# A new written order of all steps, pinned on five engines instead of three, in a decaying linear attention followed by a gated convolution

## The chip, the cores and the metric

The kernel runs on one core of one Trainium2 chip. The metric is the device time of one execution in microseconds. Three runs of the kernel before took 331.88, 332.5 and 334.31 us, a median of 332.5 us. One more execution was profiled; durations, waits and windows come from that one.

## What is computed

The first half is a linear attention with a complex decay for 4 batches, 8 heads, 768 time steps and a head dimension of 48. The second half treats the 8 x 48 = 384 outputs of a time step as channels, runs a causal convolution of 5 taps over them as a gate, and multiplies the gate into a projection:

```python
mag = np.sqrt(a_re * a_re + a_im * a_im)
scale = np.minimum(mag, 0.999) / (mag + 1e-06)
a_re_n, a_im_n = (a_re * scale, a_im * scale)
for t in range(S):
    ar, ai = (a_re_n[:, :, t, :, None], a_im_n[:, :, t, :, None])
    new_re = ar * S_re - ai * S_im
    new_im = ar * S_im + ai * S_re
    kv = np.einsum('bhd,bhe->bhde', k[:, :, t], v[:, :, t])
    S_re, S_im = (new_re + kv, new_im)
    y[:, :, t] = np.einsum('bhd,bhde->bhe', q[:, :, t], S_re)
...
for k in range(K):
    gate_pre += conv_w[k][None, None, :] * xp[:, k:k + S, :]
gate = 1.0 / (1.0 + np.exp(-gate_pre))
val = x @ w_val
return (gate * val @ w_out).astype(np.float32)
```

All data is float32, except that the three weight arrays arrive as 64-bit floats.

## The kernel before, in words

The kernel does not run the recurrence step by step. It takes the logarithm of the decay, sums it along time, and turns k and q into decayed and rotated vectors of 96 components, so that the attention becomes matrix products over chunks of 128 time steps with a carried state.

**Units and chunks.** The work of the attention is cut into 10 units: 8 of a batch with four heads, of which the first and the last are split into two of two heads each. Units 0 and 1 are two heads each, units 2 to 7 four, units 8 and 9 two. A unit has six chunks of 128 steps.

**Steps.** Every stream of work is a Python generator, and a letter stands for one advance of one generator. In the order of the data:

- `L` loads one of ar, ai, k or q of a unit through SyncE (line 114, two transfers each); the seventh and eighth `L` load the raw 64-bit weights w_val and w_out (line 141). `V` loads v of a unit (line 132, three transfers).
- `W` turns the weights into float32 on VectorE with one ScalarE instruction each (lines 186 to 208); the conv weights are loaded in the course of it (line 223).
- `X` and `x` (even and odd units) prepare a unit: logarithm and exponential on ScalarE (lines 278, 282, 289, 292, 297), VectorE lines 284, 294 and 299. `R`/`r` take the arctangent (312), sum along time (249), and form the angle in turns (318, 328, 332). `A`/`a` add the sum of the logarithms (344, 348). `S` is the two sines (356, 360), `E` the two exponentials (365, 367).
- `B` multiplies k and q by the decay (379) and the rotation (382) into kx and, for q, into the tile trig; kx goes out to DRAM as kd (line 392, SyncE). There is one kx buffer, so line 382 for the next unit waits until TensorE has transposed the last.
- `N` loads half a unit of kd back as kn, with time on the partitions (line 413, three transfers, after a small GpSimd memset in line 407). `T` transposes kx and trig on TensorE (430), and ScalarE copies each result into kq (431).
- Per chunk, `s` makes the scores (457, 458), `k` masks them on VectorE (464), `y` makes the output from the carried state and the scores (477, 480) and copies it out on ScalarE (481), and `t` updates the state (494, 495, copy in 497). There is one PSUM bank for y.
- `D` moves three chunks of y of all heads of a unit into xT, the array with channels on the partitions (line 509, issued by GpSimd).
- `C` is the conv on VectorE for 128 channels of a batch (518, then 521 four times), `G` the sigmoid on ScalarE (529), `M` the projection in pieces of 384 time steps (matmuls recorded as line 255; 542 multiplies the gate in; 576 copies the result), `O` the store of 128 time steps by GpSimd (813). For the last batch the conv is done in halves, and the projection of a piece begins before the gate is there.

**Table sets.** ScalarE holds the functions of one table set at a time. `table_set` (line 104) loads another set if the last loaded one has a different name: one for logarithm and exponential (`X`, `E`), one for the trigonometric functions (`R`, `S`), one for the sigmoid (`G`). The written order of these steps therefore decides how many loads there are.

**What sets the order.** The string `ORDER` holds 991 letters. A loop calls `advance` once for each letter, then goes round a fixed list of letters until all is done. A letter whose conditions are not met does nothing:

```python
for key in ORDER:
    advance(key)
while not finished():
    assert any([advance(key) for key in "TskGMBEASRXaxrCWtyDONVL"])

before = {}
for ins in nc.cur_bb.bb.instructions:
    if ins.engine not in IN_ORDER:
        continue
    if ins.engine in before:
        tc.add_manual_dep(
            ins, before[ins.engine].name,
```

The framework under the kernel chooses the order of an engine's instructions itself where nothing ties them. The last loop ties every instruction of an engine in `IN_ORDER` to the one written before it on that engine, so that these engines run the written order. In the kernel before these are TensorE, ScalarE and VectorE. SyncE and GpSimd, which issue the transfers, run in the framework's order.

**Buffers that decide when a transfer may be issued.** Six buffers hold the loads (a load waits until the one six before it has been read), three hold kn, two v, two trig, one kx, four z, two xT (the raw weights use the same two), two the outputs before their store. TensorE has four general PSUM banks, two for scores, one for the state and one for y.

Of the kernel before, what the change touches and what calls it, by code (L numbers as in the profile page):

```python
# [19 lines left out]

PI = math.pi
ORDER = (
    "LLXLXxxXXVxXLxxXXxxXRxrWWWWWLRWWRrrLWLVWRARRALWrarWraARSSWWWaWWWWWrSSEWEBBBLBWXWXEENXLNWTTTWTTWT"
    "XTXTBLsskBXBWkyLWtBTskNXXLtRRxRyWskWWsWxTTxTRykWtRTxWxWxTWWTyLsWkWRtWTxytskxrrDyAttWsksARNSyktSr"
    "DVysWtrAErysWrkWDErBLatBskSatBLyLSkaNByXEWWXyNWTTtDTTTTTTLTWTTTTXTTTtEstBLXsVBktkyXWsBLkWyBskxtX"
    "yDstykWskNXytxWCCCCCTTXTyTTDTTTTxCCTCTTTTVTCTsktCxskCCLCCtNyCxCskCRRCLGMRMMsxtMykMxMyDRAARRsxrrr"
    "ktRSSMMAOMMstrEEOryMrMBLMMrSSBNyaMBLLLOaXMtkXMMaMyMEMDBTTTTTTTTTTTTXTTXTTstEBLMsNtBkykBLxsOMxsNt"
    "yVksXBkXtCysxkXtXyMxMkyxTTTyttTOCTTTTTCTTCTCMDDCOTNxTCTCTCCCCLRCCRCskRstCxCCGMMMMMMRskRtVykLRxrr"
    "rMMORsykAMSyrDMSAAEaOrskrtMrMsOaEBMtLBNykMSyMaMtSEBLLXyBNXMMTTMTTTTTTLTTTTTTTTsEtMXDBLsXBkkBLXLx"
    "txXyskCtysBXMOtCXRRyDskRxkCNtTtTVTTTTTTsxxRAyLRxCkCMANxRxrrAyMMMMOyDtTVTTTTTrTTRSSssCCktCyskCras"  # L30
    "kECtOyCCsEBkrBCCtCCyDBskCtykNCGMaMaMMyMtByMCCCMMOCCCtTDTTTTTTTMsksrtrCNCSMVMCSskMMykOMCMMEEBCOsB"
    "NsBtNMykMMCykMDyMstBTTTTTOTTkTtstykMyDssMtykkMMOtMCCyCsCksCtCCCCCCCOykDCtCCMGCCMstyMMCGMMyMkyMMt"
    "MDMOOMMMMMOCCCCCCGMMMMMMMMOOMMO"
)
IN_ORDER = (
    mybir.EngineType.PE, mybir.EngineType.Activation, mybir.EngineType.DVE
)
TURN = 2.0 ** 24
RADIAN = 2.0 * PI / 2.0 ** 32 * (1.0 - 2.0 ** -22)
# [962 lines left out]
```

## Time and profile before

| what | value |
|---|---|
| median of three runs | 332.5 us (331.88 to 334.31) |
| the profiled execution's own time | 332.24 us |
| its span, first to last instruction | 330.5 us |
| mean granted TensorE clock | 0.940 |
| moved by transfers | 53.31 MB, 161 GB/s on average |
| ScalarE table loads | 31 |

The page names engines as PE (TensorE matmuls), PEld (its weight loads), DVE (VectorE), ACT (ScalarE), POOL (GpSimd), and SPq for the queue of SyncE, which only issues transfers. A group row reads: line, engine, operation, output<-input, shapes, count, then busy us and mean ns of one, then the idle time of the engine just before those instructions and who ended it. A wait row reads: engine and line, `<-` what released it, us in total, how many times, the longest. A window row reads: start and end, its length, then for PE, PEld, DVE, ACT and POOL the busy us and the number of instructions, then the granted clock, the busy share of the transfer engines and GB/s. A timeline or chain row begins with the start and the duration in us. A row of transfer issues reads: the transfer, the queue, the count, KB each, and the median us from issue to landing.

### The profile page before, as it was taken

The page shows a single profiled execution, that of the slowest core. Times are in us where ns is not written, and L with a number is a line of the kernel's source. Part 1 is how long each engine was busy: PE and PEld are TensorE (multiplying, and loading weights), DVE is VectorE, ACT ScalarE, POOL GpSimd, SP SyncE. Part 2 cuts the span into 40 slices and gives each one's busy share as a digit, 9 for nine tenths or more (in the row PEclk, how much of TensorE's full clock was granted, in tenths as well). Part 3 has the DMA queues.
Part 4 walks back from the last instruction along what each step waited for, and adds up shares of the span by engine and source line. Part 5 has one row for each costly group of instructions (what it writes and reads, how often), then busy time and mean ns, then how long its engine had stood idle before and what let it go on. Part 6 is the DMA issues. An engine that isn't in the chain of part 4 may idle for free.

```text
span 330.5 us, 8134 instructions
## 1 busy us (share of the span) xinstructions
PE 263.2 (80%) x3234; PEld 204.1 (62%) x3234; DVE 257.4 (78%) x341; ACT 245.9 (74%) x455; POOL 59.8 (18%) x148
## 2 busy tenths in 40 slices
PE   0030775747999899989969999899998999999950
PEld 0030664635998487668868887698696756866520
DVE  4499889999698999968968999689789857294500
ACT  5729879999979789998849899989894474552110
POOL 3000001121033022030430030303303312132110
PEclk9999959785999799999969999999999999999995
DMA  7994989839999722788989025997424504321120
GB/s 198 279 244 100 264 235 241 173 91 285 237 322 168 195 77 69 236 227 225 278 224 189 3 68 194 246 275 184 122 57 126 137 18 125 84 86 32 60 78 0
DMA packets 87804, 53.31 MB, mean 161 GB/s; under 512 B 36432, under 2 KB 84816, under 8 KB 87760
## 3 DMA queue, kind: packets, MB, share of 16 engines
q1 hardware_dynamic: 83664, 43.28, 50.8%
q0 software_dynamic: 4096, 9.44, 9.4%
q8 instruction: 27, 0.44, 0.6%
q14 instruction: 17, 0.14, 0.1%
HBM read 33.83 MB, written 14.16 MB: 145 GB/s over the span
## 4 chain that ended last, share of the span: by engine, by line
PE 31%; DVE 23%; ACT 14%; issue 12%; DMA 11%; POOL 3%; SPq 2%; POOLq 0%; DVEq 0%; ACTq 0%
PE pt L430 9%; PE pv L255 6%; PE po L255 4%; DMA kn<-kd 4%; ACT L104 3%; PE sc_ps L457 3%; DVE sm L464 3%; PE y_ps L480 3%; DMA raw<-in_moe_w_val_dram 3%; DVE main L379 3%; DMA kd<-kx 3%; DVE main L249 2%; DVE main L318 2%; DMA xT<-y_sb 2%; PE y_ps L477 2%
## 5 line engine op out<-in xcount | busy, mean ns | idle before, releaser
L431 ACT COPY kq<-pt 96x384 f32<-96x384 f32 x128 | 52.0, 508 | 4.7 <-PE pt L430 4.5
L509 POOL DMA_DIRECT2D xT<-y_sb x80 | 41.0, 519 | 77.4 <-ACT y_sb L481 74.9
L521 DVE SCALAR_TENSOR_TENSOR z<-xT,cw_sb,z 128x768 f32<-128x768 f32 (+1 forms) x60 | 51.4, 856 | 1.7
L255 PE MATMUL pv<-xT,wv_sb 128*64 128x384 f32 x288 | 51.4, 499 | 0.0
L255 PE MATMUL po<-wo_sb,z 128*64 128x384 f32 x288 | 51.2, 488 | 0.0
L430 PE MATMUL pt<-ident,kx 128*96 128x128 f32 x192 | 37.2, 308 | 10.4 <-DVE kx L382 9.5
L464 DVE TENSOR_TENSOR sm<-sc_ps,mask 128x512 f32<-128x512 f32 (+1 forms) x60 | 34.6, 578 | 13.0 <-PE sc_ps L458 9.0
L480 PE MATMUL y_ps<-sm,v_in 128*48 128x128 f32 x384 | 41.5, 279 | 3.1 <-DVE sm L464 3.1
L457 PE MATMUL sc_ps<-kq 96*64 96x128 f32 x384 | 42.4, 281 | 1.8 <-DVE sm L464 1.7
L458 PE MATMUL sc_ps<-kq 96*64 96x64 f32 x384 | 42.3, 227 | 0.0
L477 PE MATMUL y_ps<-kq,S_sb 96*48 96x128 f32 x320 | 36.3, 286 | 7.2 <-ACT y_sb L481 4.1
L104 ACT ACT_TABLE_LOAD x31 | 39.8, 1283 | 1.3 <-PEq L986 0.8
L430 PE MATMUL pt<-ident,trig 128*96 128x128 f32 x192 | 36.5, 305 | 4.5 <-DVE trig L382 2.8
L458 PEld LDWEIGHTS sc_ps<-kq 96*64 96x64 f32 x384 | 38.5, 140 | 1.7
L255 PEld LDWEIGHTS pv<-xT,wv_sb 128*64 128x64 f32 x288 | 26.0, 141 | 17.6 <-issue 2.9
L457 PEld LDWEIGHTS sc_ps<-kq 96*64 96x64 f32 x384 | 32.1, 141 | 5.1 <-DVE sm L464 2.6
L255 PEld LDWEIGHTS po<-wo_sb,z 128*64 128x64 f32 x288 | 24.6, 136 | 15.4 <-DVE z L542 1.6
L481 ACT COPY y_sb<-y_ps 112x256 f32<-112x256 f32 (+1 forms) x60 | 19.5, 326 | 19.6 <-PE y_ps L480 19.0
L430 PEld LDWEIGHTS pt<-ident,kx 128*96 128x96 f32 x192 | 23.5, 142 | 15.2 <-issue 11.7
L477 PEld LDWEIGHTS y_ps<-kq,S_sb 96*48 96x48 f32 x320 | 21.3, 125 | 15.1 <-ACT y_sb L481 6.4
L480 PEld LDWEIGHTS y_ps<-sm,v_in 128*48 128x48 f32 x384 | 27.1, 126 | 4.1 <-DVE sm L464 3.9
L494 PE MATMUL S_ps<-v_in,kn 128*64 128x48 f32 x320 | 27.7, 225 | 1.6 <-ACT S_sb L497 1.6
(84 smaller groups left out, 484.5 us busy)
## 6 DMA issues: line engine op xcount, KB each, us to landing
kd<-kx SPq DMA_DIRECT2D x12, 576.0 KB, 5.0
out_dram<-ot POOLq DMA_DIRECT2D x24, 192.0 KB, 2.5
ar_in<-in_a_re_dram SPq DMA_DIRECT2D x12, 288.0 KB, 4.3
ai_in<-in_a_im_dram SPq DMA_DIRECT2D x12, 288.0 KB, 4.7
k_in<-in_k_dram SPq DMA_DIRECT2D x12, 288.0 KB, 4.1
q_in<-in_q_dram SPq DMA_DIRECT2D x12, 288.0 KB, 4.1
xT<-y_sb POOLq DMA_DIRECT2D x48, 72.0 KB, 3.3
v_in<-in_v_dram SPq DMA_DIRECT2D x16, 144.0 KB, 4.9
```

Source lines behind the costliest of these rows:

```text
L104: nc.scalar.preload_act_table_set(name)
L255: nc.tensor.matmul(out[c:c + 64], lhsT[:, c:c + 64], rhs, **kw)
L430: nc.tensor.transpose(pt[:C2, j, :], src[:, j, f, h, :], ident)
L431: nc.scalar.copy(tj[:, s, f], pt[:C2].rearrange("c j p -> c p j"))
L457: nc.tensor.matmul(sc[lo:lo + half, h, :], k[:, :half], q, start=True, stop=True)
L458: nc.tensor.matmul(sc[hi:hi + half, h, half:], k[:, half:], q[:, half:], start=True, stop=True)
L464: nc.vector.tensor_tensor(out=two(sm), in0=two(sc[:, :g]), in1=mask[:, :, None, :].to_broadcast([C, 2, g // 2, C]), op=ALU.mult)
L477: nc.tensor.matmul(o, self.S_sb[n - 1][:, h * D:(h + 1) * D], self.part(1, h, n), start=True, stop=False)
L480: nc.tensor.matmul(o, vt[:, h, n], sm[:, h, :], start=(n == 0), stop=True)
L494: nc.tensor.matmul(S_all[:64, cols], kn[:, c0:c0 + 64], vt[:, h, n], **at_h)
L509: XQ.dma_start(out=xTs[b][c0 % P:c0 % P + c2 - c0, c0 // P, EXT + hf * HS:EXT + (hf + 1) * HS], in_=self.y[hf][r0:r0 + c2 - c0, h // 2],)
L521: nc.vector.scalar_tensor_tensor(out=z, in0=xT[:, c, EXT + t0 - t:EXT + t0 - t + n], scalar=cw_sb[:, TAPS - 1 - t, c:c + 1], in1=z, op0=AL ...
```

## The change

The whole string `ORDER` is replaced by another one of the same length, with the same number of each letter, and `IN_ORDER` gains SyncE and GpSimd. Nothing else in the kernel differs: the code of every step, the tiles and the buffers are the same, but steps stand in another order, and the transfers of SyncE and GpSimd are issued in the written order too.

```diff
 ORDER = (
-    "LLXLXxxXXVxXLxxXXxxXRxrWWWWWLRWWRrrLWLVWRARRALWrarWraARSSWWWaWWWWWrSSEWEBBBLBWXWXEENXLNWTTTWTTWT"
-    "XTXTBLsskBXBWkyLWtBTskNXXLtRRxRyWskWWsWxTTxTRykWtRTxWxWxTWWTyLsWkWRtWTxytskxrrDyAttWsksARNSyktSr"
-    "DVysWtrAErysWrkWDErBLatBskSatBLyLSkaNByXEWWXyNWTTtDTTTTTTLTWTTTTXTTTtEstBLXsVBktkyXWsBLkWyBskxtX"
-    "yDstykWskNXytxWCCCCCTTXTyTTDTTTTxCCTCTTTTVTCTsktCxskCCLCCtNyCxCskCRRCLGMRMMsxtMykMxMyDRAARRsxrrr"
-    "ktRSSMMAOMMstrEEOryMrMBLMMrSSBNyaMBLLLOaXMtkXMMaMyMEMDBTTTTTTTTTTTTXTTXTTstEBLMsNtBkykBLxsOMxsNt"
-    "yVksXBkXtCysxkXtXyMxMkyxTTTyttTOCTTTTTCTTCTCMDDCOTNxTCTCTCCCCLRCCRCskRstCxCCGMMMMMMRskRtVykLRxrr"
-    "rMMORsykAMSyrDMSAAEaOrskrtMrMsOaEBMtLBNykMSyMaMtSEBLLXyBNXMMTTMTTTTTTLTTTTTTTTsEtMXDBLsXBkkBLXLx"
-    "txXyskCtysBXMOtCXRRyDskRxkCNtTtTVTTTTTTsxxRAyLRxCkCMANxRxrrAyMMMMOyDtTVTTTTTrTTRSSssCCktCyskCras"
-    "kECtOyCCsEBkrBCCtCCyDBskCtykNCGMaMaMMyMtByMCCCMMOCCCtTDTTTTTTTMsksrtrCNCSMVMCSskMMykOMCMMEEBCOsB"
-    "NsBtNMykMMCykMDyMstBTTTTTOTTkTtstykMyDssMtykkMMOtMCCyCsCksCtCCCCCCCOykDCtCCMGCCMstyMMCGMMyMkyMMt"
-    "MDMOOMMMMMOCCCCCCGMMMMMMMMOOMMO"
+    "XLXLLXXXXxxXxXxxRLxRRxWRWWWLAWRWLRxrALWLWrrAWWRSSErrWEBVBLNaXBLXraWBTaNWWrSSWWWWTWTWVTXTTTETWsWW"
+    "sXXWWkskstEBBLWWyXWBBWkWTWLLWtXtXRRRWyWkWtTWxxxTNTLTytWtskRRRAWxxytTTxRyxAskWTskNyDxryskAStrrskD"
+    "SsWykrrarWEtWrVytEBWLSDBtskStBLNLBaLysNakTXyXTTTETTTTTTTTWTWTTETBLsWyDtWsXBkktWyXstyWBLVsXksyNDx"
+    "BtXTTkTTkystXyTkWxWCCCCTTyDXCTVTtTTxTNTTCTTsskRykstCtCCxCxCCCsLCkyCCtRCRCGMMMtxMkMRAAMRxyDttRsxr"
+    "rMrAsRSMSMrOEMkLyrMrMOaMEBLMOBMkarSaBSByLLTXMNyMXMTTTLMTTTTTTTTTTEENTTsMXXsMXtkDyBMsLBkyktsyBLtx"
+    "NksxVCBkystkCMTTytxxTODtXTyDCCVXCTTCxTMMtTTMLXTxTTCLCTTTxOCCTsCCCkCCRRRNCstCOCGMMMMMRkMRysRtMxrr"
+    "ryAMAsRkSAMtOrarSEskrykaDMEBLMMMrBayMBLSyBtMNMMSXMNsLLETTMTTTTTTXkyTDTTTTTTXtXETBLssktyXsktytsBk"
+    "XkBLxxtOBXyNXRsRCtyskkTTCTTVtxRTTTTyCOMxxyDMRTOTNRTLTVRTCTRCxTTsskkDtyxsktAxrrsCrtSykSAMALEEBBNs"
+    "BBraaMrNOyMyMstTTaMCCrDkCTTrTTTCkCSCTtyCCtCCCOCGMMMyMDCssktMskSECVMtyskCEBMstCCCMOBNCNykMyBMMkys"
+    "MtBTTDCTkOTTTTTtCCyMMyCDtMskstMMMstkMykCMsMOtyMMOystkMsOMDMCCCCtCCytCCCCkCCkCMMMCCCGMOCCMGyMMMyM"
+    "MODMOMMMMMOCCCCCCMGMMMMOMMOMMOM"
 )
 IN_ORDER = (
-    mybir.EngineType.PE, mybir.EngineType.Activation, mybir.EngineType.DVE
+    mybir.EngineType.PE, mybir.EngineType.Activation, mybir.EngineType.DVE, mybir.EngineType.SP, mybir.EngineType.Pool
 )
```

## The prediction

> **What bounds the kernel now.** I read the page's busy shares first, then the busy time by stage, then who waits for whom on each engine, then the chain that ended last, and SyncE's queue.
>
> ```profile
> PE 263.2 (80%) x3234; PEld 204.1 (62%) x3234; DVE 257.4 (78%) x341; ACT 245.9 (74%) x455; POOL 59.8 (18%) x148
> ```
>
> Three engines lie within 18 us of each other, so no single one is the bound. The stages (start:end, length, then busy time and instructions of PE, PEld, DVE, ACT, POOL, then granted clock, share and rate of the transfers) say which limits where:
>
> ```profile
> 0.00:20.00 20.00, 0.09 (x2) 0.12 (x4) 10.79 (x20) 11.42 (x17) 3.24 (x23) 1.00 0.91 253
> 20.00:45.00 25.00, 11.93 (x105) 10.17 (x107) 23.29 (x39) 18.92 (x35) 0.11 (x1) 0.94 0.73 187
> 45.00:80.00 35.00, 21.98 (x279) 18.29 (x277) 33.40 (x47) 34.50 (x57) 4.17 (x12) 0.79 0.75 202
> 80.00:260.00 180.00, 171.37 (x2294) 138.26 (x2294) 158.24 (x176) 154.37 (x282) 37.84 (x84) 0.96 0.68 176
> 260.00:310.00 50.00, 49.60 (x514) 32.98 (x512) 30.01 (x60) 25.22 (x63) 12.81 (x25) 1.00 0.29 84
> ```
>
> Up to 80 us VectorE and ScalarE set the pace: TensorE works 34 us of 80, while from 45 to 80 ScalarE has only 0.5 us of slack in 35. From 80 to 260 the three are busy 95%, 88% and 86% of the time, and what one loses in a wait the others lose soon after. From 260 to 310 TensorE alone is full (49.6 of 50). An order of steps can't make an engine's work less, so it is the waits that it can win or lose. These are the ones that matter (engine and line, what released it, us in total, times, longest); first VectorE from 80 to 280, then the rows of the whole span:
>
> ```profile
> DVE kx L382 <- PE pt L430: 8.5, 3, 2.9
> DVE z L518 <- DMA xT<-y_sb: 6.3, 3, 2.8
> ```
> ```profile
> DVE z L518 <- DMA xT<-y_sb: 11.5, 4, 5.1
> PE S_ps L495 <- DMA kn<-kd: 4.9, 2, 2.9
> PE y_ps L477 <- ACT y_sb L481: 4.1, 4, 1.8
> DVE cvt L186 <- DMA raw<-in_moe_w_val_dram: 2.5, 1, 2.5
> ```
>
> The conv's first instruction (L518) waits for the transfer of y into xT, the product kx (L382) waits until TensorE has read the one kx buffer, S waits for kn, and y waits until its one PSUM bank is copied out.
>
> **The change, part by part.** Walking the letters of both strings through the conditions in the code gives the written order on each engine; for the old string this gives 31 table loads, which is what the trace has. Instruction kinds and counts are equal in both strings, except for table loads. Distances below are sums of mean durations from these rows (busy, mean ns):
>
> ```profile
> L104 ACT ACT_TABLE_LOAD x31 | 39.8, 1283 | 1.3 <-PEq L986 0.8
> L521 DVE SCALAR_TENSOR_TENSOR z<-xT,cw_sb,z 128x768 f32<-128x768 f32 x36 | 36.6, 1015 | 0.9
> L464 DVE TENSOR_TENSOR sm<-sc_ps,mask 128x512 f32<-128x512 f32 x36 | 24.6, 685 | 2.2 <-PE sc_ps L458 2.2
> L284 DVE TENSOR_TENSOR main<-tmp,ai_in 128x1152 f32<-128x1152 f32 x6 | 8.1, 1352 | 0.4 <-ACT tmp L282 0.4
> L299 DVE SCALAR_TENSOR_TENSOR main<-main,tmp 128x1152 f32<-128x1152 f32 x6 | 8.1, 1349 | 0.0
> L379 DVE TENSOR_TENSOR main<-main,k_in 128x1152 f32<-128x1152 f32 x6 | 8.1, 1350 | 0.0
> ```
>
> (a) *Four more table loads.* The new string gives 35 loads: the ln, trig and ln again of units 0 and 1 are no longer taken together (seven loads in its first 91 letters, three in the old string's), and 28 follow in both. 4 x 1.283 = 5.1 us more on ScalarE, all before the last of unit 0's transposes, which the trace has at 38.16. What hides them: ScalarE is idle 20.00 - 11.42 + 25.00 - 18.92 = 14.7 us up to 45 us, of which less than 4 pass before the first data (L278 at 3.99), so over 10.7 are left. The cover is real but is itself a wait on VectorE, and after 45 us there is none. Bounds 0 and +5.1; I take one load uncovered, +1.3, nearer the free end because the idle time is twice the cost.
>
> ```profile
> 3.99 0.68 ACT L278 ACTIVATE main<-ar_in 128x576 f32<-128x576 f32 x1 [1.89 <-DMA ar_in<-in_a_re_dram]
> ...
> 26.30 0.76 ACT L360 ACTIVATE trig<-trig,b_quart 128x576 f32<-128x576 f32 x1
> 27.07 1.28 ACT L104 ACT_TABLE_LOAD   x1
> ...
> 28.37 0.68 ACT L365 ACTIVATE main<-main 128x576 f32<-128x576 f32 x1
> ...
> 38.16 0.63 PE L430 MATMUL pt<-ident,trig 128*96 128x128 f32 x3
> ```
>
> From the end of L360 (27.06) to the start of L365 (28.37) a switch takes 1.31 us, the load and nothing else. The Trainium skill, ScalarE: Activation LUTs, section What ACT_TABLE_LOAD costs, speaks against the change more strongly: it adds a drain of about 1380 ns to each switch, 2.66 us in all. By that page four switches would be 10.6 us, an estimate; the rows here don't agree with it, and the sum goes by them.
>
> (b) *Conv further behind its transfer.* From the last xT issue to the conv of chunks 1 of batch 0, 1, 2 and of the second half of chunk 0 of batch 3, the old order has 1.4, 1.4, 0.6 and 0.9 us of VectorE work. The new one has 5.1, 5.7, 10.4 and 6.8. For batch 0: one L284 before (1.35); now one L299, one L521, one L284 and two L464, 1.349 + 1.015 + 1.352 + 2 x 0.685 = 5.1. The transfer's landing:
>
> ```profile
> 101.47 4.17 DMA xT<-y_sb
> ...
> 238.73 2.46 DMA xT<-y_sb
> ```
>
> 5.1 us covers even the 4.17, so the 6.3 us of waits between 80 and 280 should go. The fourth wait (5.1 us, near 306) lies where TensorE is full and counts nothing; nor can the last half's conv be moved, it still has nothing ahead of it. How much of 6.3 reaches the end: none if TensorE or ScalarE was as late, all if VectorE alone paced the stage. With all three about equally busy I take half, -3.2; bounds 0 and -6.3.
>
> (c) *kx further behind the transposes that free it.* For units 3, 5 and 7 VectorE had 1.3, 1.3 and 2.1 us between the last transpose of the unit before and L382 (for unit 3 one L379, 1.35). Now it is 3.0, 3.4 and 3.5: 1.7 + 2.1 + 1.4 = 5.2 us more, against 8.5 us of waits in three places. Half again: -2.6; bounds 0 and -8.5. What is late next there is TensorE's first transpose of the new unit, which now follows kx and its twin at once.
>
> (d) *TensorE's own waits.* Between kx and the first S, unit 5 (whose S has the 2.9 us wait) gets 2.0 us more VectorE work (12.7 to 14.7, from the same means), unit 0, with the other 2.0, only 0.3. Pairs of outputs y with nothing or one short step of TensorE (S or scores) between go from five to one. I count 2.0 of the 4.9 + 4.1 us as covered; half, -1.0; bounds 0 and -9.0.
>
> (e) *SyncE and GpSimd pinned, loads moved.* In the trace SyncE did not run the old string's order: conv_w's loads went out at 24 us, far ahead of their letter, and loads were put between the pieces of kn.
>
> ```profile
> 7.44 4.58 SPq L132 DMA_DIRECT2D v_in<-in_v_dram  x3
> 12.06 0.62 SPq L141 DMA_DIRECT2D raw<-in_moe_w_out_dram  x1
> ...
> 24.16 2.68 SPq L223 DMA_DIRECT2D raw_cw<-in_moe_conv_w_dram  x5
> ...
> 35.43 0.38 SPq L413 DMA_DIRECT2D kn<-kd  x1
> 35.86 0.48 SPq L114 DMA_DIRECT2D q_in<-in_q_dram  x1
> ```
> ```profile
> SPq L413 <- DMA kn<-kd: 33.6, 17, 4.3
> ```
> ```profile
> raw<-in_moe_w_out_dram SPq DMA_DIRECT2D x1, 1152.0 KB, 8.3
> ```
>
> Pinned, the three pieces of a kn stand together, and whatever is behind waits for kd to land and for a piece to land (up to 4.3 us). Behind unit 2's kn stands k of unit 4, which VectorE needs 55 us of its work later; conv_w, now at its letter, has 9.7 us of VectorE work between load and use, unit 0's v 13.1. So 0; bounds 0 and +4.3. Unit 0's v moves behind the loads of unit 2, and the 1152 KB of w_out go out up to 4.6 us earlier, right behind w_val, for which VectorE already waits 2.5 us. Unit 0's v is 2 heads x 768 x 48 x 4 bytes = 288 KB; if w_out and w_val shared the engines, 1152 - 288 = 864 KB more at 253 GB/s is 3.4 us; if first come is first served, nothing. I take +0.5, as w_val already had 288 KB of v behind it; bounds 0 and +3.4. On GpSimd an output store now stands ahead of the last xT transfer of all:
>
> ```profile
> L813 POOL DMA_DIRECT2D out_dram<-ot x24 | 13.4, 560 | 54.5 <-ACT ot L576 48.3 <-ACT S_sb L497 4.8 <-DVE main L379 0.8
> ```
>
> 0.56 us at most, and the final conv and projection wait for it: +0.3.
>
> **The sum.** +1.3 - 3.2 - 2.6 - 1.0 + 0.5 + 0.3 = -4.7 us. The profiled execution took 332.24 us (span 330.5), within 0.3 of the runs' median 332.5. 332.2 - 4.7 = **327.5 us**, 1.5% under the median.
>
> **The rivals.** *The waits only move (333).* What VectorE gains, TensorE's full stretch at the end takes back: from 260 us it is 49.6 of 50 busy, and if the work that it lacks before 260 is not ready sooner, the end stays. For it: each wait above was counted on one engine alone. Against it: up to 80 us TensorE has 46 us idle and would take work sooner. Then b, c and d are 0 and the rest (+1.3, +0.5, +0.3) is in part covered: 332.2 to 334.3, the middle being 333.
>
> *The table loads reach the path (337.3).* One mechanism, before 45 us: a load stands ahead of the exp that unit 0 or 1 needs, so kx, the transposes and all behind them come later by it, and the 0.5 us of slack from 45 to 80 can't make it up. All four: 332.2 + 5.1 = 337.3, if nothing else is won. It decides once the uncovered part is 3.6 us more than the gains of b to d (335.8, 1% over the median, less 332.2): with all four uncovered, while the gains stay under 1.5. For it: the 34.50 us of 35. Against it: 10.7 us of idle time up to 45. By the skill's 2.66 us the price would be 10.6 us, an estimate from that page.
>
> *All the covered waits count (319).* b and c in full, d's 2: 332.2 - 6.3 - 5.2 - 2.0 + 0.3 = 319.0. For it: the chain goes through xT twice. Against it: the engines' near-equal load.
>
> *The pins do nothing* can be ruled out for SyncE by the raw_cw row; that they cost nothing is in the forecast.
>
> **How the numbers follow.** Forecast 49%, waits only move 22%, table loads on the path 17%, all waits 12%. The forecast's own range is 323 to 331; a tenth of it lies above 329.2, 1% under the median, which is about what a measurement of this kernel can tell from no change. Faster by over 1%: 0.44 + 0.12 = 0.56; within 1%: 0.22 + 0.05, less 0.02 beyond 335.8, is 0.25; slower: 0.17 + 0.02 = 0.19. The range of 320 to 337.5 leaves out most of the fourth case and the far end of the third (all four loads and a late kn).
>
> **What would show it.** Right: 35 table loads; the row of L518 waiting for xT under 6 us, with only the last half's wait left (about 5); L382 waiting for pt about 3 us instead of 8.5; the stage 80 to 260 with VectorE busier than 88%. If (a) is right, ScalarE's busy time before 45 us is up by 5 with the idle time down by about as much, and unit 2's transposes start no later than 80. Wrong: VectorE waiting as long as before for other releasers in place of xT and pt (the first rival); unit 2's transposes starting after 83 us (the second); new waits for kn, w_val or conv_w of more than 3 us (e).

## The result and the profile after

The changed kernel takes 348.59 us (median of 4 runs, 347.49 to 351.07) against 333.12 us for the kernel before (4 runs, 331.88 to 334.31): a ratio of 1.052, 95% interval 1.047 to 1.057. It is slower by 5%, where 1.5% faster was forecast, and outside the range. The profiled execution took 347.98 us, its span is 346.3. Ratios, here and below, leave out the few executions that ran more than 1.5% above the fastest of their kernel (one took 909 us); the medians are of all executions.

The same stages as in the prediction, of the kernel after:

```profile
0.00:20.00 20.00, 1.55 (x16) 1.28 (x16) 12.12 (x23) 14.85 (x21) 3.33 (x22) 1.00 0.92 274
20.00:45.00 25.00, 14.81 (x126) 12.02 (x127) 24.52 (x42) 23.77 (x41) 0.18 (x2) 0.87 0.54 136
45.00:80.00 35.00, 22.60 (x232) 18.07 (x231) 29.11 (x36) 29.34 (x48) 3.79 (x9) 0.70 0.71 174
80.00:260.00 180.00, 162.09 (x2159) 130.43 (x2161) 147.07 (x162) 149.57 (x274) 33.41 (x77) 0.95 0.68 177
```

Up to 45 us every engine has done more than before: VectorE 36.6 us in place of 34.1, ScalarE 38.6 in place of 30.3, of which 6.4 are five more table loads (eight in place of three; one of the five came at 45.57 before). Then the lead is lost. From 45 to 80 VectorE and ScalarE, which had been full, are idle 5.9 and 5.7 us (1.6 and 0.5 before), and from 80 to 260 VectorE works 147.1 us where it worked 158.2. The engines' waits (whole span) show what they lack:

```profile
ACT main L278 <- DMA ar_in<-in_a_re_dram: 10.3, 5, 3.5
PE S_ps L495 <- DMA kn<-kd: 6.8, 3, 3.7
DVE z L518 <- DMA xT<-y_sb: 6.3, 3, 5.1
DVE main L284 <- DMA ai_in<-in_a_im_dram: 4.3, 2, 3.8
```

The two waits that the new order was to shorten are shorter: xT is 6.3 us in place of 11.5, and L382 waiting for the transposes, 8.5 us before, is down to 0.3 in the answer for 80 to 260 us. New are loads that come late: ar, for which ScalarE waits 10.3 us in place of 3.0, and ai, for which VectorE waits 4.3 in place of 0.6. Loads come from SyncE, and its queue has changed most. The waits of the queue itself:

```profile
SPq L413 <- DMA kn<-kd: 66.7, 20, 5.6
SPq L392 <- DVE kx L382: 50.1, 4, 18.9
...
SPq L413 <- DMA kd<-kx: 6.2, 4, 2.0
```

It stood 33.6 us behind pieces of kn before; now it stands 66.7, once for each of the 20 half units, 3.3 us on average. Part of this is only another place to wait: before, the same line also waited 22.8 us for kd to land, and now 6.2, so the two rows together grow from 56.4 to 72.9 us. The row of the kernel before:

```profile
SPq L413 <- DMA kd<-kx: 22.8, 13, 3.8
```

The queue after, in order of time:

```profile
43.43 1.24 SPq L392 DMA_DIRECT2D kd<-kx  x2
44.72 1.44 SPq L114 DMA_DIRECT2D ar_in<-in_a_re_dram  x2
46.20 1.19 SPq L114 DMA_DIRECT2D ai_in<-in_a_im_dram  x2
47.43 1.05 SPq L114 DMA_DIRECT2D k_in<-in_k_dram  x2
48.53 6.63 SPq L413 DMA_DIRECT2D kn<-kd  x3
55.26 1.12 SPq L114 DMA_DIRECT2D q_in<-in_q_dram  x2
56.48 4.64 SPq L413 DMA_DIRECT2D kn<-kd  x3
63.20 1.99 SPq L132 DMA_DIRECT2D v_in<-in_v_dram  x3
```

From 48.5 to 61.1 the queue issues six pieces of kn and the two transfers of one q. And this is in the chain that ended last:

```profile
48.53 5.32 DMA kn<-kd
53.87 0.63 SPq L413
54.54 2.88 DMA kn<-kd
57.42 0.14 issue
57.56 0.34 PE S_ps L495 x2
```

The first piece lands after 5.3 us, only then does SyncE issue the second and third, these land 2.9 us later, and TensorE's S, which waited for them, starts at 57.56. From 45 to 80 us ScalarE waits 2.1 us for this S, and VectorE 3.6 us for the scores behind it. Most of the rest of that hole is a load of ar that came late: ScalarE waits 2.0 us for it, and VectorE 1.9 us for ScalarE's step behind it.

### The profile page after: what moved, and what is told of

The parts are those of the page before. It is cut to its first block, busy times and chain, and to the rows that moved or that the text cites. A ratio compares the mean times of both kernels' runs of the same rounds, so it can differ in the third digit from the quotient of the medians.

```text
span 346.3 us, 8129 instructions
## 1 busy us (share of the span) xinstructions
PE 272.0 (79%) x3234; PEld 208.2 (60%) x3234; DVE 259.7 (75%) x341; ACT 251.4 (73%) x460; POOL 58.7 (17%) x148
## 4 chain that ended last, share of the span: by engine, by line
PE 23%; DVE 18%; ACT 18%; DMA 14%; issue 14%; SPq 7%; POOL 3%; POOLq 0%; ACTq 0%; DVEq 0%
DMA kn<-kd 7%; PE pt L430 6%; PE pv L255 4%; ACT kq L431 4%; ACT L104 3%; SPq L114 3%; SPq L132 3%; PE sc_ps L457 3%; DVE z L521 3%; DMA ar_in<-in_a_re_dram 2%; DVE main L379 2%; DVE kx L382 2%; DMA raw<-in_moe_w_val_dram 2%; DMA v_in<-in_v_dram 2%; PE po L255 2%
## 5 line engine op out<-in xcount | busy, mean ns | idle before, releaser
L255 PE MATMUL po<-wo_sb,z 128*64 128x384 f32 x288 | 52.4, 497 | 0.9 <-DVE z L542 0.8
L255 PE MATMUL pv<-xT,wv_sb 128*64 128x384 f32 x288 | 49.9, 487 | 0.0
L457 PE MATMUL sc_ps<-kq 96*64 96x128 f32 x384 | 44.2, 291 | 2.5 <-DVE sm L464 2.5
L464 DVE TENSOR_TENSOR sm<-sc_ps,mask 128x512 f32<-128x512 f32 (+1 forms) x60 | 34.1, 578 | 15.7 <-PE sc_ps L458 12.9
L458 PE MATMUL sc_ps<-kq 96*64 96x64 f32 x384 | 44.6, 233 | 0.0
L480 PE MATMUL y_ps<-sm,v_in 128*48 128x128 f32 x384 | 42.2, 286 | 1.0 <-DMA v_in<-in_v_dram 0.5
L458 PEld LDWEIGHTS sc_ps<-kq 96*64 96x64 f32 x384 | 40.7, 146 | 2.0 <-issue 0.7
L494 PE MATMUL S_ps<-v_in,kn 128*64 128x48 f32 x320 | 30.0, 232 | 8.5 <-ACT S_sb L497 6.5
L457 PEld LDWEIGHTS sc_ps<-kq 96*64 96x64 f32 x384 | 33.0, 148 | 5.9 <-DVE sm L464 3.3
L255 PEld LDWEIGHTS po<-wo_sb,z 128*64 128x64 f32 x288 | 23.8, 138 | 17.4 <-issue 2.7
L494 PEld LDWEIGHTS S_ps<-v_in,kn 128*64 128x64 f32 x320 | 26.0, 147 | 12.3 <-ACT S_sb L497 8.3
L495 PE MATMUL S_ps<-v_in,kn 128*33 128x48 f32 x320 | 24.7, 217 | 6.8 <-DMA kn<-kd 6.8
```

The lines of the kernel that those rows point to most:

```text
L255: nc.tensor.matmul(out[c:c + 64], lhsT[:, c:c + 64], rhs, **kw)
L457: nc.tensor.matmul(sc[lo:lo + half, h, :], k[:, :half], q, start=True, stop=True)
L458: nc.tensor.matmul(sc[hi:hi + half, h, half:], k[:, half:], q[:, half:], start=True, stop=True)
L464: nc.vector.tensor_tensor(out=two(sm), in0=two(sc[:, :g]), in1=mask[:, :, None, :].to_broadcast([C, 2, g // 2, C]), op=ALU.mult)
L480: nc.tensor.matmul(o, vt[:, h, n], sm[:, h, :], start=(n == 0), stop=True)
L494: nc.tensor.matmul(S_all[:64, cols], kn[:, c0:c0 + 64], vt[:, h, n], **at_h)
```

## The experiments

Two theories stood against each other at first: that pinning SyncE costs the time (P), or that the new order of the computing engines is worse by itself (O). The first four kernels undo one part each; ratios are to the kernel before on the same chip.

**The order alone.**

```diff
-    mybir.EngineType.PE, mybir.EngineType.Activation, mybir.EngineType.DVE, mybir.EngineType.SP, mybir.EngineType.Pool
+    mybir.EngineType.PE, mybir.EngineType.Activation, mybir.EngineType.DVE
```

> The new order with only TensorE, ScalarE and VectorE pinned; SyncE and GpSimd in the framework's order as before. Theory P (pinning SyncE puts the pieces of kn together, 20 waits of 3.3 us that nothing may pass, and loads behind them come late): the time falls to 327 to 335 us, the SyncE wait for a kn piece falls from 66.7 to about 34 us. Theory O (the new order of the computing engines is worse by itself: four more table loads, other distances): 343 to 349 us with the SyncE wait at about 34.

Measured: 330.09 us (10 runs), ratio 0.993 (0.990 to 0.997). The new order is a little faster than the old, by less than 1%. In SyncE's queue the wait for a piece of kn is 19.4 us, less than the 34 that were expected:

```profile
SPq L413 <- DMA kd<-kx: 29.9, 13, 4.0
SPq L413 <- DMA kn<-kd: 19.4, 16, 2.4
```

O falls; TensorE, ScalarE and VectorE run the same sequence of instructions here as in the changed kernel. That allows the two profiled executions to be laid side by side, and the loss is seen to grow over the whole span, not in one hole: the changed kernel starts the last product of unit 2 (L382) 4.9 us later (77.25 against 72.36), that of unit 4 10.7 later (147.52 against 136.81), that of unit 7 12.4 later (232.45 against 220.07), and the last piece's matmuls 16.7 later (322.55 against 305.88).

**The pins alone.** The old string, `IN_ORDER` with all five engines.

> The old order with SyncE and GpSimd pinned too. Theory P: 342 to 352 us, and the SyncE wait for a kn piece rises from 33.6 to over 60 us. Theory O: 331 to 336 us, whatever SyncE's queue shows.

Measured: 351.95 us, ratio 1.061 (1.052 to 1.070). SyncE's row agrees with the changed kernel's:

```profile
SPq L413 <- DMA kn<-kd: 67.7, 20, 5.6
```

**The new order with SyncE pinned, and with GpSimd pinned.** Each has one of the two added engines in `IN_ORDER`.

> The new order with SyncE pinned and GpSimd in the framework's order. Theory P: within 2 us of the changed kernel (346 to 351). If GpSimd's pin is the cause instead: 327 to 335. Theory O: 346 to 351 as well.

> The new order with GpSimd pinned and SyncE in the framework's order. Theory P: like the run with the order alone, 327 to 335. GpSimd's pin as the cause: 343 to 349. Theory O: 343 to 349.

Measured: with SyncE 352.84 us, ratio 1.058 (1.049 to 1.068); with GpSimd 330.05 us, ratio 0.996 (0.992 to 1.000). The first lies above the 346 to 351 that were expected if SyncE's pin was the cause; its interval overlaps the changed kernel's (1.047 to 1.057), so the pin of SyncE alone gives the whole loss in the new order, and GpSimd's pin alone costs nothing that can be seen. In the old order the two pins were only tried together.

**Taking the wait away.** A kn has three pieces: the first half of the heads for all 128 rows, then the other half in two pieces of 64 rows. They write different columns, but of one tile, and in the kernel's instructions the second piece carries a wait for the first, which the rows show as 20 waits, one for each half unit. With the two halves of the heads in tiles of their own, the pins and the order stay and the wait goes:

```diff
-        flat = qkp.tile([C, HN * g * C2 + 1], F32, name="kn", bufs=KNB)
...
-        for h in (0, g // 2):
-            cols = slice(h * C2, (h + g // 2) * C2)
+        for h in (0, m):
+            flat = qkp.tile([C, HN * m * C2 + 1], F32, name=f"kn{h > 0:d}", bufs=KNB)
...
+            cols = slice(h * C2, (h + m) * C2)
             for i0, i1, n in rows(h, g):
-                nc.sync.dma_start(out=kn[i0:i0 + n, :, cols], in_=src[i1:i1 + n, :, cols])
+                nc.sync.dma_start(out=kn[i0:i0 + n], in_=src[i1:i1 + n, :, cols])
```

The state's matmuls read the tile of their head, and the small memset is done twice.

> The changed kernel with kn in two tiles, one for each half of the heads, so that the second piece no longer waits for the first to land; order and all five pins stay. Theory P1 (the queue loses its time in the 20 waits of a piece for the piece before it): the waits of 66.7 us go and the time falls to 328 to 336 us. Theory P2 (the written order of the loads, or the wait of each transfer for the eighth one before it, costs as much without them): 340 to 348.

> The old order, all five engines pinned, kn in two tiles. Theory P1: 330 to 337 us, where the old order with pins took 352. Theory P2: 343 to 352.

Measured: 331.90 us with the new order, ratio 1.001 (0.998 to 1.004), and 332.21 with the old, ratio 0.999 (0.996 to 1.002). With the old order the whole loss is gone, with the new all but some 2 us against the order alone (330.09). The two rows on kd and kn that are left in SyncE's queue with the new order (line 415 is line 413 shifted by the edit):

```profile
SPq L415 <- DMA kd<-kx: 4.8, 5, 2.0
...
SPq L114 <- DMA kn<-kd: 1.0, 2, 0.6
```

P1 holds: the pin does its harm through this wait. The difference of the ratios 1.001 and 0.993, less than 1%, is what the pins and the second tile together still cost in the new order; the written order of the loads is one candidate for it, not tested by itself.

**The same split without the pins.**

> The new order with three engines pinned and kn in two tiles. The framework already puts other loads between the pieces, so theory P1 expects little, 327 to 331 us against 330 without the split. If SyncE's piece waits (19 us left) still reach the path: under 327.

> The old order with three engines pinned and kn in two tiles. Theory P1 expects 329 to 333 us against 332; the piece waits of 33.6 us go, and TensorE's waits for kn (4.9 us) fall below 3.

Measured: 334.05 us with the new order, ratio 1.005 (1.001 to 1.009), and 331.79 with the old, ratio 0.999 (0.995 to 1.002). With the old order nothing changes, though 33.6 us of waits go (and TensorE's wait for kn falls from 4.9 to 2.2, as expected): where other loads may pass, the wait was free. With the new order it came out slower than without the split, 334 against 330, outside what was expected. The framework orders SyncE's transfers anew when the tiles differ; which of these moves costs the 4 us was not tried.

**Letting others pass, with the wait left in.** All five engines pinned, one kn tile, but the second and third piece are written behind the next step of SyncE:

```diff
+                if h:
+                    later.append((kn[i0:i0 + n, :, cols], src[i1:i1 + n, :, cols]))
+                else:
+                    nc.sync.dma_start(out=kn[i0:i0 + n, :, cols], in_=src[i1:i1 + n, :, cols])
...
+        if key in "LV":
+            rest_of_kn()
```

> The changed kernel, all five engines pinned, with the second and third piece of each kn written behind SyncE's next load or store instead of right behind the first; the wait of a piece for the piece before it stays. If what counts is that nothing may pass the waiting piece: SyncE's piece waits fall from 66.7 to 25 to 45 us and the time to 333 to 341. If the wait itself delays S, whatever passes: 345 to 349.

Measured: 336.38 us, ratio 1.011 (1.007 to 1.015). The piece waits fell less than expected, as often only one load stands between (line 424 holds the moved pieces; this profiled execution took 337.3 us):

```profile
SPq L424 <- DMA kn<-kd: 50.7, 19, 4.7
```

Still, most of the loss is gone while three quarters of the waiting is left: what stands behind a waiting piece counts for more than the sum of the waits. As the sum fell too, this run alone does not part the two; the old order without pins, where 33.6 us of waits went and the time stayed, points the same way.

**The four table loads.** The order alone, with ScalarE functions that need another table set replaced in units 0 and 1, so that four loads fall away:

```diff
-        nc.scalar.activation(mf[:, 1], mf[:, 1], AF.Arctan)
+        nc.scalar.activation(mf[:, 1], mf[:, 1], AF.Arctan if u else AF.Abs)
...
+        if u != 1:
+            table_set("trig_and_small")
```

> The new order with three engines pinned, and unit 0's arctangent and unit 1's two sines replaced by absolute values, so that four table loads before 45 us fall away (31 are left); the angles of these two units are therefore not computed. If the loads reach the path: 325 us, 5.1 under the 330.1 of the order alone. If ScalarE's idle time covers them: 329 to 331. The prediction's one load in four: 328.8.

Measured: 330.20 us, ratio 0.995 (0.992 to 0.999), against 330.09 and 0.993 with all loads. ScalarE's busy time up to 45 us falls by 4.9 us, from 37.9 to 33.1, and the time does not. The four loads cost nothing that can be seen: ScalarE's idle time before 45 us covers them.

**The conv further behind its transfer, alone.** In the old string `CCCC` is moved behind the `D` that feeds the next chunk, for batch 0 so:

```diff
-txWCCCCCTTXTyTTDTTTTxCC
+txWCTTXTyTTDCCCCTTTTxCC
```

> The old order with three engines pinned, four conv letters of chunk 0 in each of batches 0, 1 and 2 moved behind the transfers for chunk 1, so that 4.6 to 5.4 us of VectorE work stand between transfer and conv in place of 0.6 to 1.4. The row of L518 waiting for xT should fall from 11.5 to about 5. The prediction's half share: 329.3 us against 332.5, ratio 0.990. Waits only move: ratio 0.997 to 1.003.

Measured: 332.53 us, ratio 1.001 (0.997 to 1.005). The wait for xT fell only from 11.5 to 9.5 us, not to 5, so this does not show what its full removal would bring. What it shows is that 2 us less of this wait are not 2 us less of time; half of them, 1 us, would lie at the edge of the interval (0.997).

## Why the prediction was wrong, point by point

**Step (e) failed**, and it alone gave the wrong sign. It named the place (three pieces together, everything behind them held up) and priced it as 0, with an upper bound of +4.3 us: nobody would wait for what the queue delayed. Measured: +20 us for both pins with the old order (351.95 against 332.35), +23 us with the new (352.84 with SyncE pinned against 330.09). Three errors are in that one step.

- The bound. 4.3 us was the longest single wait of a row that holds 17 of them. A wait that recurs is bounded by its count: 20 half units times a landing. The pieces that are waited for are of 96 to 288 KB, and the list of issues of before has their landing, 3.4 to 4.3 us, here its two ends:

```profile
kn<-kd SPq DMA_DIRECT2D x16, 96.0 KB, 3.4
kn<-kd SPq DMA_DIRECT2D x6, 192.0 KB, 4.3
```

  So 68 to 86 us of standing queue were in reach; 66.7 were measured. Such a bound is not a price: a quarter to a third of it was paid in time. The row's 33.6 us was no measure either, because the framework's order had put loads between the pieces.
- The cover. The step looked for the consumers of three loads, the nearest with 9.7 us of VectorE work between load and use, and concluded that nobody waits. It left out what else stands in the queue: the store of kd, the loads of ar and ai, and the later pieces of kn themselves. In the changed kernel kx of unit 1 is finished at 38.91 (37.55 + 1.36), but its kd goes out at 43.43, behind kn of unit 0 and v; with kn in two tiles it goes out at 39.07, where kx is finished at 39.04. Behind this kd stand the ar that ScalarE waits 2.0 us for and the kn that S of unit 1 at 57.56 waits for.
- The rivals. The slower case was given to the table loads. SyncE's queue, as a mechanism with a price of its own, was not among them.

The sign that was set for (e), new waits of more than 3 us for kn, w_val or conv_w, showed only in part: S waits for kn up to 3.7 us (2.9 before), but the largest new waits are for ar, which it did not name. Its +0.5 for w_val did not come either; VectorE waits 0.2 us for it in place of 2.5.

**The rest, read from the order alone**, where the sum of (a) to (d) was -5.5 us (+1.3 - 3.2 - 2.6 - 1.0) and -2.3 us was measured (330.09 against 332.35 on the same chip).

(a) The place was right and +1.3 too much: four loads are 5.1 us of ScalarE's time and none of the kernel's that can be seen. The count was one short: the trace has 36 table loads, not 35. The last stands at line 360, between the two sines of the last unit, where the new order puts sigmoids (at 276.94 us in the changed kernel); what it costs was not tested. (b) and (c) were right as to the waits and wrong as to what they are worth. VectorE's waits in the order alone, from 80 to 260 us:

```profile
DVE sm L464 <- PE sc_ps L458: 9.1, 6, 4.2
DVE main L284 <- ACT tmp L282: 4.0, 1, 4.0
DVE main L379 <- DMA q_in<-in_q_dram: 2.2, 1, 2.2
...
DVE kx L382 <- PE pt L430: 0.3, 1, 0.3
```

The xT wait in this stretch is gone (6.3 us before), the kx wait is down from 8.5 to 0.3, and in their place VectorE waits 9.1 us for scores (2.2 before) and 4.0 us for ScalarE (0.4). The stage tells the balance:

```profile
45.00:80.00 35.00, 24.81 (x254) 19.01 (x252) 32.25 (x42) 34.67 (x59) 4.66 (x11) 0.78 0.70 186
80.00:260.00 180.00, 170.74 (x2324) 135.93 (x2324) 159.66 (x177) 155.64 (x286) 37.38 (x84) 0.99 0.66 176
```

VectorE works 159.7 us of 180, where it worked 158.2: of 14.5 us of waits taken away, 1.4 are won. The first rival, that waits only move, describes this stage. As I read it, work that is put ahead of a waiting instruction is taken from somewhere else in the same engine's sequence, and where it is missing another wait opens; half was too large a share for that. What the order does win shows early: unit 2's last product (L382 for q) starts at 72.36 in place of 76.99. Of these 4.6 us 2.4 are left at unit 7 (220.07 against 222.48) and 0.5 at the last piece's matmuls (305.88 against 306.41) in the two profiled executions (331.89 and 332.24 us, so the first is 1.8 above its kernel's median). Which of the moved steps makes the early lead was not taken apart, nor (d) tested by itself.

The +0.3 for GpSimd's pin in (e) fits: nothing that can be measured (330.05 us with it, 330.09 without).

## What to carry to other kernels

Before a queue is made to run in written order, list what each of its instructions waits for and multiply each recurring wait by its count. That product is the bound for a queue in which nothing passes a waiting transfer; here 66.7 us of it cost some 20 us of time, and a freer order had been hiding it. Then look for waits that need not be there: two pieces of one tile that write different columns, and a second tile removed the cost. Of the versions tried, the new order with SyncE left to the framework is faster than both kernels, 330.09 us, by 0.7% against the kernel before.

## What the runs showed of the hardware

A switch of ScalarE's tables took 1.31 us from one instruction to the next in the trace of before, 1.28 of them the load itself, and four of them in idle time cost the kernel nothing that can be seen. The landing of a kn piece grows far less than its size: 48 KB take 2.4 us before and 2.3 after, 144 KB 3.5 and 3.2, 288 KB 3.6 and 5.0, so six times the bytes take about twice the time or less. A queue that had to see one piece of each half unit land before the next paid 3.3 us a time (66.7 over 20).
